# Fifteen small copies on GpSimd's queue are removed, and the hand-written order is replaced

## The chip, the cores and the metric

The kernel runs on one core of a Trainium2 chip. Such a core has a matrix engine (TensorE, PE in the profile; its weight loads are listed as PEld), three engines for elementwise work (VectorE = DVE, ScalarE = ACT, GpSimd = POOL), and SyncE (SP), which only issues transfers. Each engine takes its instructions strictly in order; engines and transfers meet only through semaphores. Transfers are issued by a queue (here POOL's, SP's and, at the very start and end, ACT's) and carried out by 16 DMA engines that all queues share. The metric is the device time of one execution in microseconds; lower is better.

## The reference

```python
B, H, S, D = 8, 12, 448, 64
scores = (q @ k.T) / sqrt(D)                  # per batch and head, 448 x 448
attn   = maximum(scores, 0) ** 2 / S          # no softmax
x      = (attn @ v) as [B*S, H*D]             # 3584 x 768
h      = x @ w_in                             # 768 -> 2048
g      = 0.5 * h * (1 + erf(h / sqrt(2)))     # exact gelu
out    = g @ w_out                            # 2048 -> 768, float32
```

All inputs are float32 in HBM; they are cast to bf16 on their way in by the transfers that POOL issues.

## The kernel before, in words

**Work.** Attention runs batch by batch (b = 0 to 7), each batch in three groups of four heads (g = 0, 1, 2), each group in seven steps of 64 keys (i = 0 to 6). One step is four matmuls `ps<-qT,kT` (L816), a relu `a_sq<-ps` (L828 on ACT or L830 on DVE) and a squaring `a_sq<-a_sq` (L838 on DVE). After the seven steps of a group come 28 matmuls `pav<-a_sq,v_sb` (L878) and two copies into `xT`. When all groups of a batch are done, the feed-forward part of that batch may start: `psh<-xT,win_sb` (L937) in 16 tiles of six matmuls for batches 0 to 3, a block form with fewer multiplications (`pb`, L1089) for batches 4 to 7, and `pso` (L1266) for the second layer of all. The feed-forward matmuls of earlier batches lie between the attention steps of later ones.

**How q and k arrive.** Scores need q and k transposed. For batches 0 and 1 TensorE does that (`tp`, L705 to L712). For batches 2 to 7 the path is: POOL issues a load of one group into `nq` (L511) or `nk` (L602); when it has landed SP issues a DMA transpose (L739) from `nq` into `qT`, or from `nk` into `kT`; for q the two halves of partitions are then also swapped into a second place, by DVE (two copies, L563) or by SP (two transfers, L760 and L761). `nq` and `nk` have four slots (NN = 4) and a batch takes three, so the load of a group overwrites a slot that a group of the batch before has used; `war` finds the transposes that must have read it.

**The gates.** `add_gate(b, g)` puts a copy of 128x16 values from `qT` to a tile `gate` that nobody reads on POOL (L784). It waits until the q transpose of group g of batch b has landed (for b = 2 until the swapped copy is made), and as POOL works in order, everything behind it in POOL's queue waits too. There are 15, for batches 2 to 6.

**What sets the order.** The string `ORDER` (L89) lists all work in one sequence: a letter for the engine (P = PE, A = ACT, D = DVE, G = POOL, S = SP) and the number of the operation in the order in which the program's text adds it; `Z1056` is a matmul of zeros, 1056 columns in all (L1601). `place` follows the list. So the list decides which engine does a relu, a copy or a swap where there is a choice, and in which order each engine's queue stands. The framework then adds the waits that the data need, and a wait of each POOL transfer for the eighth one ahead of it.

## Time and profile before

| | |
|---|---|
| median of 3 runs | 365.86 us (364.35 to 365.88) |
| the profiled execution | 366.48 us |
| its span, first to last instruction | 364.6 us |
| PE busy | 354.6 us (97%) |
| DVE busy | 297.8 us (82%) |
| ACT busy | 205.5 us (56%) |
| POOL busy | 67.0 us (18%) |
| granted TensorE clock | 1.00 |
| loads through POOL's queue | 22.47 MB, 42.8% of 16 DMA engines |
| SP's queue, transposes above all | 20.03 MB, 28.6% of 16 DMA engines |

The table is read from the first execution that the profiler recorded, which was 0.62 us longer than the median of the three runs. The share of an engine is a mean over stages that differ: until about 25 us TensorE waits for relus and copies, from there it is nearly always busy. The transfers of q, k and v go on until about 200 us; afterwards only outputs are stored.

### The profile page before, as it was taken

The page shows a single profiled execution, that of the slowest core. Times are in us where ns is not written, and L with a number is a line of the kernel's source. Part 1 is how long each engine was busy: PE and PEld are TensorE (multiplying, and loading weights), DVE is VectorE, ACT ScalarE, POOL GpSimd, SP SyncE. Part 2 cuts the span into 40 slices and gives each one's busy share as a digit, 9 for nine tenths or more (in the row PEclk, how much of TensorE's full clock was granted, in tenths as well). Part 3 has the DMA queues.
Part 4 walks back from the last instruction along what each step waited for, and adds up shares of the span by engine and source line. Part 5 has one row for each costly group of instructions (what it writes and reads, how often), then busy time and mean ns, then how long its engine had stood idle before and what let it go on. Part 6 is the DMA issues. An engine that isn't in the chain of part 4 may idle for free.

```text
span 364.6 us, 8274 instructions
## 1 busy us (share of the span) xinstructions
PE 354.6 (97%) x3439; PEld 222.0 (61%) x3439; DVE 297.8 (82%) x510; ACT 205.5 (56%) x333; POOL 67.0 (18%) x102
## 2 busy tenths in 40 slices
PE   8799999999999899999999999999999999999995
PEld 4464544555544455554455555899977887787663
DVE  3999878869999779999977999987866576767764
ACT  4999665546678585777966766425634025235000
POOL 8666173111723024052000000000000000000000
PEclk9999999999999999999999999999999999999999
DMA  9999999999899999999955301020101002402324
GB/s 175 201 200 200 184 172 178 191 197 207 134 173 177 144 232 166 196 173 224 192 132 72 91 2 45 2 62 27 42 6 43 2 8 80 131 0 61 99 58 131
DMA packets 72085, 43.87 MB, mean 120 GB/s; under 512 B 36336, under 2 KB 68720, under 8 KB 72048
## 3 DMA queue, kind: packets, MB, share of 16 engines
q0 software_dynamic: 32032, 22.47, 42.8%
q1 hardware_dynamic: 39120, 20.03, 28.6%
q10 hardware_dynamic: 896, 0.85, 0.7%
q8 instruction: 27, 0.44, 0.5%
q14 instruction: 10, 0.08, 0.1%
HBM read 45.61 MB, written 11.01 MB: 155 GB/s over the span
## 4 chain that ended last, share of the span: by engine, by line
PE 63%; DMA 21%; DVE 5%; ACT 4%; issue 3%; POOL 2%; SPq 0%; POOLq 0%; DVEq 0%
PE pso L1266 27%; PE pb L1089 18%; DMA nq<-in_q_dram 9%; PE psh L937 7%; DMA qT<-nq 7%; PE ps L816 5%; PE pav L878 4%; ACT a_sq L828 4%; DMA kT<-nk 4%; DVE a_sq L838 2%; DMA nk<-in_k_dram 2%; PE spin L1445 1%; DVE osb L1300 1%; DVE qT L563 1%; POOL wout_sb L532 1%
## 5 line engine op out<-in xcount | busy, mean ns | idle before, releaser
L828 ACT ACTIVATE a_sq<-ps 128x896 bf16<-128x896 f32 x126 | 110.5, 925 | 36.5 <-PE ps L816 36.2
L838 DVE TENSOR_TENSOR a_sq<-a_sq 128x896 bf16<-128x896 bf16 x169 | 96.4, 615 | 2.0 <-ACT a_sq L828 1.6
L937 PE MATMUL psh<-xT,win_sb 128*128 128x448 bf16 x384 | 76.9, 353 | 0.0
L830 DVE TENSOR_SCALAR a_sq<-ps 128x896 bf16<-128x896 f32 (+1 forms) x43 | 46.2, 1076 | 15.9 <-PE ps L816 15.6
L937 PEld LDWEIGHTS <-win_sb 128*128 128x128 bf16 x384 | 35.6, 98 | 38.2 <-issue 7.2
L1120 DVE TENSOR_TENSOR part<-pb,part 128x448 f32<-128x448 f32 x80 | 46.9, 619 | 12.9 <-PE pb L1089 11.1
L1266 PEld LDWEIGHTS <-s_sb 128*128 128x128 bf16 x424 | 40.4, 98 | 27.1 <-issue 3.3
L816 PE MATMUL ps<-qT,kT 64*64 64x448 bf16 (+1 forms) x700 | 47.8, 350 | 3.6 <-ACT a_sq L828 1.9
L947 ACT ACTIVATE h_sb<-psh 128x448 bf16<-128x448 f32 x64 | 34.5, 549 | 19.5 <-PE psh L937 19.5
L1266 PEld LDWEIGHTS <-h_sb 128*128 128x128 bf16 x312 | 29.9, 98 | 20.1 <-issue 2.3
L1089 PEld LDWEIGHTS <-win_sb 128*128 128x128 bf16 x384 | 36.9, 98 | 2.2
L1266 PE MATMUL pso<-t_sb,s_sb 128*128 128x384 bf16 x208 | 38.1, 326 | 0.0
L1266 PE MATMUL pso<-wout_sb,h_sb 128*128 128x384 bf16 x208 | 38.1, 326 | 0.0
L1266 PE MATMUL pso<-wout_sb,s_sb 128*128 128x384 bf16 (+1 forms) x208 | 37.7, 324 | 0.2 <-DVE osb L1300 0.2
L878 PE MATMUL pav<-a_sq,v_sb 64*64 64x448 bf16 (+1 forms) x700 | 36.1, 342 | 1.2 <-ACT a_sq L828 0.8
L1132 ACT ACTIVATE h_sb<-part 128x448 bf16<-128x448 f32 x48 | 25.2, 573 | 21.1 <-DVE part L1120 21.1
L816 PEld LDWEIGHTS <-kT 64*64 64x64 bf16 x700 | 18.3, 105 | 26.6 <-issue 18.1
L1300 DVE TENSOR_TENSOR osb<-pso,p_sb 128x384 f32<-128x384 f32 x39 | 21.5, 552 | 13.5 <-PE pso L1266 10.9
L878 PEld LDWEIGHTS <-v_sb 64*64 64x64 bf16 x700 | 20.9, 107 | 12.7 <-issue 2.2
L1089 PEld LDWEIGHTS <-ws 128*128 128x128 bf16 x288 | 27.7, 98 | 1.2
L1089 PE MATMUL pb<-xs,ws 128*128 128x224 bf16 x192 | 22.8, 259 | 0.0
L1089 PE MATMUL pb<-xs,win_sb 128*128 128x224 bf16 x192 | 22.5, 259 | 0.0
(70 smaller groups left out, 311.8 us busy)
## 6 DMA issues: line engine op xcount, KB each, us to landing
nk<-in_k_dram POOLq DMA_DIRECT2D x23, 224.0 KB, 8.1
nq<-in_q_dram POOLq DMA_DIRECT2D x23, 224.0 KB, 8.8
v_sb<-in_v_dram POOLq DMA_DIRECT2D x4, 672.0 KB, 8.9
out_dram<-osb SPq DMA_DIRECT2D x7, 336.0 KB, 3.8
v_sb<-in_v_dram POOLq DMA_DIRECT2D x10, 224.0 KB, 8.0
out_dram<-osb SPq DMA_DIRECT2D x7, 288.0 KB, 2.8
out_dram<-osb SPq DMA_DIRECT2D x8, 240.0 KB, 3.3
win_sb<-in_moe_w_in_dram POOLq DMA_DIRECT2D x8, 192.0 KB, 9.0
```

Of the source, the lines that this page charges most:

```text
L816: nc.tensor.matmul(ps[64 * j : 64 * j + 64, e, x * w : x * w + w], kT[r, g, i * 128 + 64 * j : i * 128 + 64 * j + 64], moving, start=True, ...
L828: A.activation(ar, ps, AF.Relu, scale=c_att)
L830: V.tensor_scalar(ar, ps, c_att, 0.0, op0=mybir.AluOpType.mult, op1=mybir.AluOpType.max,)
L838: V.tensor_mul(box["a2"][:, :, :used], ar, ar)
L878: nc.tensor.matmul(pav[0][o2 : o2 + 64, e, :w], get_v()[r, 2 * v_slot(b, g) + e, bass.ts(i, D)], box["a2"][r, y, o : o + w], start=(i == 0 ...
L937: nc.tensor.matmul(ph[:, x * n : x * n + n], win_sb[:, kd, bass.ts(m + x, 128)], xT[b][:, kd, c], start=(kd == 0), stop=(kd == KD - 1),)
L947: A.activation(h_ring()[:, m : m + nm, o + c.start : o + c.stop], box[0][:, :S].rearrange("p (x n) -> p x n", x=nm), AF.Gelu,)
L1089: nc.tensor.matmul(ps[name][:, z * HS : z * HS + HS], w[:, k, bass.ts(mm, 128)], right()[:, k], start=first and k == 0 and z == 0, stop=k ...
L1120: V.tensor_add(get(to), ps[name][:, :S], get(other))
L1132: A.activation(h_ring()[:, m : m + 2, o + half[c].start : o + half[c].stop], src().rearrange("p (x n) -> p x n", x=2), AF.Gelu,)
L1266: nc.tensor.matmul(box[bank][:, n0:n1], left()[:, kf], right()[:, kf, n0:n1], start=bool(need) and kf == 0, stop=kf == K2 - 1, skip_group_ ...
L1300: V.tensor_add(out()[:, n0:n1], box[bank][:, n0:n1], other()[:, n0:n1])
```

## The change

The function `add_gate`, its tile and its calls are removed, so POOL's queue holds loads alone (and the making of the identity matrix). A load still waits for the transposes that read the slot it overwrites. The numbers in `ORDER` shift by the 15 operations, and the list is also another one: on every engine much stands in another place, 33 relus go from ACT to DVE and 26 the other way, three swaps of q halves (batch 6 group 0, batch 7 groups 0 and 2) go from DVE to SP, two copies of transposed k of batch 0 go from DVE to ACT, and the matmul of zeros stands behind the first eight score operations instead of at PE's start.

```diff
 ORDER = """
-D13 G0 Z1056 A10 G1 G7 G4 A16 G108 G1461 P11 D12 P14 D15 P17 P29 P32 D18 P38 D39 P19 P21 A30 D20
...
+G0 A10 G1 G7 G108 A16 D13 G1446 P11 D12 P14 D15 P17 P29 A18 P32 A30 G3 P19 G4 A20 D33 P21 P35 P38
...
-    gate = const.tile([128, 16], BF16, tag="gate", name="gate")
-
-    def add_gate(b, g):
-
-
-        def fn(e):
-            nc.gpsimd.tensor_copy(gate, q_seg(b, 2 * g + (b == 2))[:, : SEG : SEG // 16])
-
-        deps = [Tq[b, g, 0][b == 2]]
-        pool_q.append(sch.add((("POOL", 0.2, 0.3),), fn, deps))
...
     add_T_dma(2, [[]] * 9)
-    add_gate(2, 0)
     add_wout(0)
     add_wout(1)
-    add_gate(2, 1)
     add_wout(2)
-    add_gate(2, 2)
...
                 for g in range(G):
-                    add_gate(b + 1, g)
                     add_load(b + 2, g, g + 1)
```

Three places show the new order. In the rows DMASW names the landing of a transfer that POOL issued, DMAHW of one that SP issued; DVE, PE, Activation and Pool are the engines' own counts.

**POOL, the loads of batch 4.** Before, from the gate for batch 3, group 2 to the k load of batch 4, group 1 (the last row); the big v load is that of batch 3:

```order
L784 COPY gate<-qT 128x16 [waits DMAHW4_49,Pool_49]
L620 DMA v_sb<-in_v_dram 128x6x448 [waits DMASW5_49,PE_49]
L602 DMA nk<-in_k_dram 128x2x448 [waits DMAHW0_49,DMASW6_49]
L784 COPY gate<-qT 128x16 [waits DMAHW3_49,Pool_49]
L511 DMA nq<-in_q_dram 112x4x256 [waits DMASW7_49,DMASW0_49]
L602 DMA nk<-in_k_dram 128x2x448 [waits DMAHW5_49]
L784 COPY gate<-qT 128x16 [waits DMAHW1_49,Pool_49]
L511 DMA nq<-in_q_dram 112x4x256 [waits DMASW1_49]
L784 COPY gate<-qT 128x16 [waits Pool_49]
L784 COPY gate<-qT 128x16 [waits DMAHW1_49,Pool_49]
L602 DMA nk<-in_k_dram 128x2x448 [waits DMAHW2_49,DMASW2_49]
```

The same stretch of the change, from the q load of batch 4, group 2 (which overwrites the slot of batch 3, group 1) to the v load of batch 4; the k load of batch 4, group 1 is the row before the last:

```order
L511 DMA nq<-in_q_dram 112x4x256 [waits DMAHW3_49,DMASW5_49,DMASW0_49]
L620 DMA v_sb<-in_v_dram 128x6x448 [waits DMASW6_49,PE_49]
L602 DMA nk<-in_k_dram 128x2x448 [waits DMAHW0_49,DMASW7_49]
L511 DMA nq<-in_q_dram 112x4x256 [waits DMAHW1_49]
L602 DMA nk<-in_k_dram 128x2x448 [waits DMAHW2_49,DMASW1_49]
L620 DMA v_sb<-in_v_dram 128x4x448 [waits DMASW2_49,PE_49]
```

The k load of batch 4, group 1 now stands behind loads alone; before, a gate for batch 4, group 0 stood right ahead of it.

**POOL, the first loads of batch 2.** Before, from a piece of `w_in` to the first gate; the first `nk` row is the k load of batch 2, group 0, the second that of group 1:

```order
L526 DMA win_sb<-in_moe_w_in_dram 128x3x512 [waits DMASW3_49]
L527 DMA win_sb<-in_moe_w_in_dram 64x3x512 [waits DMASW4_49]
L528 DMA win_sb<-in_moe_w_in_dram 64x3x512 [waits DMASW5_49]
L602 DMA nk<-in_k_dram 128x2x448 [waits DMASW6_49]
L602 DMA nk<-in_k_dram 128x2x448 [waits DMASW7_49,DVE_49,Activation_49]
L526 DMA win_sb<-in_moe_w_in_dram 128x3x512 [waits DMASW0_49]
L527 DMA win_sb<-in_moe_w_in_dram 64x3x512 [waits DMASW1_49]
L528 DMA win_sb<-in_moe_w_in_dram 64x3x512 [waits DMASW2_49]
L784 COPY gate<-qT 128x16 [waits DVE_49]
```

In the change the k load of batch 2, group 0 is the first row here, and the same piece of `w_in` comes behind it:

```order
L602 DMA nk<-in_k_dram 128x2x448 [waits DMASW5_49]
L620 DMA v_sb<-in_v_dram 128x2x448 [waits DMASW6_49]
L511 DMA nq<-in_q_dram 112x4x256 [waits DMASW7_49]
L526 DMA win_sb<-in_moe_w_in_dram 128x3x512 [waits DMASW0_49]
L527 DMA win_sb<-in_moe_w_in_dram 64x3x512 [waits DMASW1_49]
L528 DMA win_sb<-in_moe_w_in_dram 64x3x512 [waits DMASW2_49]
L602 DMA nk<-in_k_dram 128x2x448 [waits DVE_49,DMASW3_49,PE_49,Activation_49]
```

The k load of group 0 moves ahead of nine transfers: two pieces of `w_in` of three transfers each, two q loads and a v load. 30 transfers stood ahead of it in POOL's queue, now 21.

**ACT, the first relu of batch 2.** Its queue shows where PE's first score step of batch 2 stands, since each gelu `h_sb<-psh` follows one feed-forward tile on PE. Before, the relu of that step is the last row but one; thirteen gelus stand ahead of it in the whole queue:

```order
L947 ACTIVATE h_sb<-psh 128x448
L828 ACTIVATE a_sq<-ps 128x896
L947 ACTIVATE h_sb<-psh 128x448
L565 CAST xT<-pav 128x448 x2
L947 ACTIVATE h_sb<-psh 128x448 x6
L828 ACTIVATE a_sq<-ps 128x896 x2
L947 ACTIVATE h_sb<-psh 128x448
```

In the change the relu of the first step is DVE's, and that of the second step, which follows it directly on PE, is the `a_sq` row behind the two copies:

```order
L936 ACTIVATE h_sb<-psh 128x448
L817 ACTIVATE a_sq<-ps 128x896 x2
L936 ACTIVATE h_sb<-psh 128x448
L817 ACTIVATE a_sq<-ps 128x896
L565 CAST xT<-pav 128x448 x2
L817 ACTIVATE a_sq<-ps 128x896
L936 ACTIVATE h_sb<-psh 128x448
```

On PE ten feed-forward tiles stand ahead of the first score step of batch 2 instead of thirteen.

## The prediction

> **What bounds the kernel now.** I read the page first, then PE's waits, then the chain of waits, then the queues behind it. The page's first part, and the table of stretches:

> ```profile
> PE 354.6 (97%) x3439; PEld 222.0 (61%) x3439; DVE 297.8 (82%) x510; ACT 205.5 (56%) x333; POOL 67.0 (18%) x102
> ```
> ```profile
> 100.00:120.00 20.00, 20.00 (x197) 9.96 (x196) 19.58 (x34) 15.80 (x24) 5.94 (x9) 1.00 1.31 168
> 120.00:126.00 6.00, 4.70 (x52) 2.24 (x49) 4.72 (x8) 3.42 (x7) 0.00 (x0) 1.00 1.36 152
> 126.00:140.00 14.00, 13.99 (x134) 7.16 (x138) 10.61 (x18) 9.54 (x15) 5.43 (x9) 1.00 1.09 212
> 140.00:170.00 30.00, 29.55 (x318) 15.66 (x314) 28.86 (x51) 22.10 (x31) 7.88 (x15) 1.00 1.31 192
> 200.00:230.00 30.00, 29.84 (x309) 16.24 (x308) 29.79 (x56) 20.82 (x29) 0.00 (x0) 1.00 0.17 46
> ```

> After the stretch and its length the columns are PE, PEld, DVE, ACT and POOL busy, clock, DMA share. TensorE is the bound: 364.6 - 354.6 = 10.0 us idle in the whole span, at full clock. The change takes no matmul away, so it can gain only what PE idles or what PE spends thinly at the start. The one stretch with visible idle time in the middle is 120 to 126 us (1.30 us). DVE is the second bound: 1.14 us idle in 140 to 170, 0.21 us in 200 to 230. PE's waits:

> ```profile
> PE ps L816 <- ACT a_sq L828: 1.9, 5, 0.5
> PE ps L816 <- DMA kT<-nk: 1.3, 1, 1.3
> PE pav L878 <- ACT a_sq L828: 0.8, 2, 0.4
> PE pav L878 <- DVE a_sq L838: 0.4, 1, 0.4
> ```

> Columns: total us, times, longest. These are 4.4 of the 10.0 us; most of the rest lies ahead of the first matmul and behind the last, where only sums and stores are left. The chain of waits leads into the one DMA wait:

> ```profile
> 84.78 5.14 DMA qT<-nq
> ...
> 97.70 8.92 DMA qT<-nq
> ...
> 106.74 0.02 POOL gate L784
> 106.76 0.49 issue
> 107.25 5.71 DMA nk<-in_k_dram
> 112.97 0.02 issue
> 112.98 12.98 DMA kT<-nk
> ```

> Start, length. The gate for batch 4, group 0 waits for a transpose until 106.74; the k load of batch 4, group 1 stands behind it, lands at 112.96, its transpose at 125.97, and at 126.01 the first scores of that group start late.

> **The change part by part.** All terms are against the profiled execution's 366.48 us (span 364.6 us), 0.62 us above the median.

> *The gates themselves.* POOL's queue with two of them, before batch 4's loads:

> ```profile
> 90.04 3.42 POOL L784 COPY gate<-qT 128x16 bf16<-128x16 bf16 x1 [13.02 <-DMA qT<-nq]
> ...
> 106.74 0.24 POOL L784 COPY gate<-qT 128x16 bf16<-128x16 bf16 x1 [9.07 <-DMA qT<-nq]
> 107.25 0.70 POOL L602 DMA_DIRECT2D nk<-in_k_dram  x1 [0.27 <-issue]
> ```

> A copy of 0.2 us on an engine that is 18% busy costs PE nothing; what counts is the idle time in brackets, in which POOL issued no load.

> *The wait at 126 us.* In the new queue the k load of batch 4, group 1 stands behind loads that wait for transposes of batch 3, the last of which lands near 90 us (84.78 + 5.14 = 89.92). With four more loads ahead at about 0.7 us of issue each it goes out near 94 instead of 107.25. Its transpose then lands 13 us earlier, near 113 at the same lengths. PE wants it at 124.7 (126.01 - 1.30) or some 2 us sooner, since the new list puts three fewer tiles ahead of it. Ten us of cover: the wait goes. Gain 1.3 us, between 0 (if what follows waits instead) and 1.74, the wait of the weight load of the same step:

> ```profile
> 126.01 0.14 PEld L816 LDWEIGHTS <-kT 64*64 64x64 bf16 x8 [1.74 <-DMA kT<-nk]
> ```

> *What is late next.* Time gained at 126 has to be kept up by DVE. It has 3.39 us to spare in 126 to 140, then almost none to 170. The new list gives DVE seven relus more on balance and takes three swaps (two copies each), two copies of kT and six copies to xT from it:

> ```profile
> L830 DVE TENSOR_SCALAR a_sq<-ps 128x896 bf16<-128x896 f32 x42 | 45.5, 1086 | 15.5 <-PE ps L816 15.2
> L563 DVE COPY qT<-qT 64x896 bf16<-64x896 bf16 x28 | 12.1, 434 | 2.3 <-DMA qT<-nq 1.6
> L563 DVE CAST xT<-pav 128x448 bf16<-128x448 f32 x8 | 4.8, 616 | 0.3 <-ACT xT L565 0.3
> L563 DVE COPY kT<-tp 128x896 bf16<-128x896 bf16 x5 | 3.1, 616 | 0.0
> ```

> 7 x 1.09 = 7.6 against 6 x 0.43 + 2 x 0.6 + 6 x 0.62 = 7.5 us: an even exchange over the run, but the copies of kT leave the first 10 us, so about 1.2 us more come later. Where DVE has no idle time that lands on PE. Of the 1.3 us I take 0.5 back; bounds 0 and 1.2 + 1.1 = 2.3 (the later work, and DVE's idle time of 140 to 170 if it has to fall somewhere).

> *The swaps on SP.* Three more swaps are two transfers each on SP (0.5 to 0.6 us of issue) and make SP wait for the transpose ahead of them:

> ```profile
> 179.43 0.55 SPq L760 DMA_DIRECT2D qT<-qT  x1
> 180.03 0.59 SPq L761 DMA_DIRECT2D qT<-qT  x1
> ...
> 186.18 175.41 SPq L1220 DMA_DIRECT2D out_dram<-osb x44
> ```

> Behind them stand later transposes of batches 6 and 7. Before, SP is through with all transposes at 186.1, when PE is still in batch 6 (by its place in the list, the step at 197.70 in the rows of the chain below is the first of batch 7). Three swaps at 1.1 us plus a landing of about 5 us (the 5.14 above) push them by 8 at most: cost nothing, cover 10 us.

> *The start of batch 2.* This is the tightest place, because the new list wants it sooner. Rows of SP, PE and the weight loads:

> ```profile
> 32.52 1.32 SPq L739 DMA_TRANSPOSE qT<-nq  x1
> 40.59 3.14 SPq L739 DMA_TRANSPOSE kT<-nk  x2
> ```
> ```profile
> 32.52 10.79 DMA qT<-nq
> ```
> ```profile
> 49.00 0.33 PEld L816 LDWEIGHTS <-kT 64*64 64x64 bf16 x12 [0.37 <-DMA kT<-nk]
> ```
> ```profile
> 126.58 1.24 PE psh L937 x6
> ...
> 172.33 3.52 PE psh L937 x18
> ...
> 197.70 0.69 PE ps L816 x12
> ```

> Now the scores of batch 2 start at 49.00, just as the transpose of k lands (0.37 us wait). A feed-forward tile is 3.52 / 3 = 1.17 us; with three fewer ahead, and small moves besides, PE comes there near 45.1. The k load moves up by nine transfers, so its transpose no longer waits for the load until 40.59; it follows that of q, at 33.8. If both take the 10.8 us that the q transpose took among loads, k lands at 44.6: no wait. If the second adds a further 2 us to the first, 46.6: 1.5 us wait. I take 0.6 us; bounds 0 and 3.9 (k lands at 49 as now). [...]

> *The first microseconds.*

> ```profile
> 4.70 0.62 ACT L565 CAST nq<-q 112x512 bf16<-112x512 f32 x1 [1.44 <-DMA q<-in_q_dram]
> ...
> 7.32 1.73 ACT L828 ACTIVATE a_sq<-ps 128x896 bf16<-128x896 f32 x2 [1.59 <-PE ps L816]
> ```
> ```profile
> 5.13 0.64 PE L1601 MATMUL fill<-zero 64*64 64x512 bf16 x3
> 5.69 0.37 PE L705 MATMUL tp<-ident,nq 112*128 112x112 bf16 x4
> ```

> Without the zeros at the start the first transposes begin when the cast ends, 5.32 instead of 5.69: 0.37 us. ACT then works without a break, as in 15 to 20 us:

> ```profile
> 15.00:20.00 5.00, 3.91 (x79) 2.39 (x82) 4.80 (x10) 5.00 (x10) 3.52 (x5) 1.00 1.39 196
> ```

> It gets two copies of kT (about 0.4 and 0.8 us); the first fits into its 1.59 us of waiting, the second does not, but one half copy to xT (about 0.4 us) leaves. Sum -0.37 + 0.8 - 0.4: 0. I take -0.2 for one more score step done by then (0.19 us); bounds -0.6 and +0.8.

> *Changes between attention and feed-forward on PE.* A tile by itself takes 1.24 us and one of a row of three 1.17 (both in the rows of the chain above), so three single tiles take 0.2 us more than a row of three, which has two pairs of changes fewer: about 0.1 us a pair. The list has 89 changes instead of 87, one pair more: +0.1.

> *Sum.* -1.3 + 0.5 + 0 + 0.6 - 0.2 + 0.1 = -0.3 us on 366.48, so 366.2; less 0.62, about **365.6 us** as a median. I call anything within 0.5% (1.8 us) no change, about what a measurement of this kernel can tell.

> **The rivals.**
> *Faster: the new list also fits better.* Without gates the loads have more room, and a list made for that may close the other small waits too. For it: the ten us of cover at 126. Against it: the two long rows of PE's waits are for ACT and DVE, which loads don't touch. The price: the 1.3 us kept in full and half of the 1.9 + 0.8 + 0.4 us: 1.3 + 1.6 = 2.9, so 363.0.
> *Slower: loads stretch the transposes.* The gates kept loads off while transposes ran (5.14 us); beside loads they take 8.92 to 12.98. At batch 2 there is no slack at all: if k's transpose lands no sooner than now, PE waits 3.9 us instead of the 0.6 in my sum, 365.6 + 3.3 = 368.9. It decides from a landing later than about 47.5. Against it: the k load is moved up by about 9 us. [...]
> *Slower: DVE takes over.* If the 2.3 us of its upper bound land on PE: 365.6 + 1.8 = 367.4, and with an uneven exchange between 140 and 230 us more, about 368.
> *No effect: a load takes the gate's place.* POOL is in order, and the new queue has early loads that wait for transposes too: the k load of batch 3, group 1 waits for that of batch 2, group 0, where the first gate stood. Then the loads start again when they did; 365.9, inside my forecast.

> **How the numbers follow.** No change (mine and the last rival) 0.37; faster 0.31; slower by the transposes 0.20; slower by DVE 0.12. The likeliest, 365.6, is the prediction. Its own range is 364.1 to 367.6. For 8 in 10 it reaches to the faster rival, 362.7, and to the slower one, 368.9.

> **What would show it.** Right: no PE wait for kT near 124 us, the k load of batch 4, group 1 out before 100 us, DVE above 95% from 126 to 170, first scores of batch 2 between 45 and 47 us with a wait under 1.5 us, the last transpose before 195 us. Wrong: PE waits of several us for kT or qT of batch 2 or 6, waits for DVE of more than 2 us in sum, or a first feed-forward tile (27.2 us now) that moves by more than 1 us.

## The result and the profile after

| | before | after |
|---|---|---|
| median of the runs, us | 365.03 (22 runs) | 366.60 (22 runs) |
| lowest and highest, us | 364.24, 365.88 | 365.14, 371.94 |
| profiled execution, us (its span) | 366.48 (364.6) | 368.19 (366.4) |

The ratio after to before is 1.0047, with a 95% interval from 1.0027 to 1.0068: slower by half a per cent, where 0.2% faster (365.6 us) was forecast. The time lies inside the range of 362.7 to 368.9. This ratio leaves out the runs more than 1.5% above the fastest of their kernel, five here, though these turn out below to be the kernel's own doing. The spread is the first thing to see: the kernel before stays within 1.7 us, the changed one takes 365.1 to 366.7 us in 13 runs and 368.2 to 371.9 in the other 9.

The first part of the page after, the stretches that the prediction showed (the same columns: stretch, length, PE, PEld, DVE, ACT and POOL busy, clock, DMA share, GB/s) with one more, 45 to 50 us:

```profile
PE 355.9 (97%) x3439; PEld 221.1 (60%) x3439; DVE 298.6 (82%) x504; ACT 204.2 (56%) x333; POOL 59.8 (16%) x87
```
```profile
45.00:50.00 5.00, 4.17 (x60) 1.80 (x62) 4.27 (x9) 3.88 (x7) 1.90 (x3) 1.00 1.24 153
100.00:120.00 20.00, 20.00 (x199) 10.00 (x196) 18.85 (x32) 13.99 (x23) 4.07 (x6) 1.00 1.44 142
120.00:126.00 6.00, 5.90 (x60) 2.71 (x54) 5.56 (x10) 3.91 (x7) 1.64 (x3) 1.00 1.42 134
126.00:140.00 14.00, 13.20 (x116) 6.48 (x116) 12.28 (x20) 10.44 (x17) 1.35 (x2) 1.00 1.32 219
140.00:170.00 30.00, 29.38 (x312) 15.47 (x316) 27.62 (x47) 19.83 (x27) 9.01 (x13) 1.00 1.23 200
200.00:230.00 30.00, 30.00 (x314) 15.92 (x307) 28.59 (x52) 22.32 (x32) 0.84 (x1) 1.00 0.36 77
```

TensorE now idles visibly at 45 to 50 us (0.83) and about 126 to 141 us; DVE has more room than before in 140 to 170 and 200 to 230 us. TensorE's waits (total us, times, longest) say for what:

```profile
PE ps L805 <- DMA kT<-nk: 2.3, 3, 1.1
PE ps L805 <- ACT a_sq L817: 1.2, 3, 0.4
PE ps L805 <- DVE qT L563: 1.1, 2, 0.8
PE pav L867 <- ACT a_sq L817: 0.4, 1, 0.4
```

The waits for ScalarE have shrunk (1.9 to 1.2, and 0.8 to 0.4). In their place stand three waits for a transpose of k instead of one, and two waits of 1.1 us in all for DVE's copies of q; these two lie at 9.4 and 15.3 us, in the new early list, and the kernel before has neither. The rows of the three waits on TensorE (start, length, the wait in brackets) are the first scores of batch 2, of batch 4, group 1, and of batch 5:

```profile
47.62 0.57 PE L805 MATMUL ps<-qT,kT 64*64 64x448 bf16 x8 [0.83 <-DMA kT<-nk]
...
126.29 0.57 PE L805 MATMUL ps<-qT,kT 64*64 64x448 bf16 x8 [0.30 <-DMA kT<-nk]
...
140.62 0.57 PE L805 MATMUL ps<-qT,kT 64*64 64x448 bf16 x8 [1.14 <-DMA kT<-nk]
```

The chain of waits now runs through DMA from 33.7 us on. First piece: the transpose of k of batch 2, group 0, and POOL let go by it. Second piece: loads and transposes of batch 4.

```profile
33.72 13.85 DMA kT<-nk
47.57 0.02 issue
47.59 0.02 POOLq L602
47.61 0.49 issue
48.10 0.73 POOL nk L602
48.83 6.35 DMA nq<-in_q_dram
```
```profile
93.14 12.62 DMA nk<-in_k_dram
105.76 0.02 issue
105.78 1.22 SPq L739
...
113.88 12.37 DMA kT<-nk
126.24 0.04 issue
126.29 0.60 PE ps L805 x8
```

POOL's queue shows what took the gates' place (start, length, idle time ahead; first the gate for batch 2, group 0 before, then the rows after):

```profile
44.20 0.65 POOL L784 COPY gate<-qT 128x16 bf16<-128x16 bf16 x1 [8.53 <-DVE qT L563]
```
```profile
48.10 0.73 POOL L602 DMA_DIRECT2D nk<-in_k_dram  x1 [8.98 <-DMA kT<-nk]
...
91.60 0.73 POOL L511 DMA_DIRECT2D nq<-in_q_dram  x1 [14.37 <-DMA qT<-nq]
...
94.57 0.73 POOL L602 DMA_DIRECT2D nk<-in_k_dram  x1
...
107.65 0.71 POOL L511 DMA_DIRECT2D nq<-in_q_dram  x1 [11.58 <-DMA qT<-nq]
```

POOL issues in order, so a load that overwrites a buffer holds everything behind it until the transpose that reads the buffer has landed: 8.98, 14.37 and 11.58 us, where the gates held 8.53, 13.02 and 9.07. The first hold ends at 48.1 instead of 44.2 us, and the loads behind it land two to three us later than those behind the gate did. The k load of batch 4, group 1 goes out at 94.57, as forecast, but lands only at 110.18, with five other loads and three transposes beside it; its own transpose takes 12.37 us beside the loads of batch 5 and lands at 126.24, where it landed at 125.97 before.

### The profile page after: what moved, and what is told of

The parts are those of the page before. It is cut to its first block, busy times and chain, and to the rows that moved or that the text cites. A ratio compares the mean times of both kernels' runs of the same rounds, so it can differ in the third digit from the quotient of the medians.

```text
span 366.4 us, 8257 instructions
## 1 busy us (share of the span) xinstructions
PE 355.9 (97%) x3439; PEld 221.1 (60%) x3439; DVE 298.6 (82%) x504; ACT 204.2 (56%) x333; POOL 59.8 (16%) x87
## 4 chain that ended last, share of the span: by engine, by line
PE 65%; DMA 22%; ACT 5%; SPq 4%; issue 2%; DVE 1%; POOL 1%; POOLq 0%
PE pso L1255 29%; PE pb L1078 18%; DMA nq<-in_q_dram 9%; DMA kT<-nk 8%; PE psh L926 6%; PE ps L805 5%; PE pav L867 4%; ACT a_sq L817 4%; DMA nk<-in_k_dram 3%; SPq L739 3%; DMA qT<-nq 2%; PE spin L1434 1%; SPq L1209 1%; DVE a_sq L827 1%; POOL wout_sb L532 1%
## 5 line engine op out<-in xcount | busy, mean ns | idle before, releaser
L817 ACT ACTIVATE a_sq<-ps 128x896 bf16<-128x896 f32 (+1 forms) x119 | 105.0, 928 | 28.5 <-PE ps L805 28.1
L819 DVE TENSOR_SCALAR a_sq<-ps 128x896 bf16<-128x896 f32 (+1 forms) x50 | 53.8, 1078 | 16.7 <-PE ps L805 16.3
L1109 DVE TENSOR_TENSOR part<-pb,part 128x448 f32<-128x448 f32 x80 | 46.9, 618 | 17.2 <-PE pb L1078 17.0
L1255 PEld LDWEIGHTS <-s_sb 128*128 128x128 bf16 x424 | 40.3, 98 | 27.2 <-issue 3.0
L805 PE MATMUL ps<-qT,kT 64*64 64x448 bf16 (+1 forms) x700 | 48.1, 350 | 5.0 <-DMA kT<-nk 2.3
L1078 PEld LDWEIGHTS <-ws 128*128 128x128 bf16 x288 | 27.7, 98 | 1.2
L511 POOL DMA_DIRECT2D nq<-in_q_dram x24 | 17.7, 739 | 54.0 <-DMA qT<-nq 40.6
L602 POOL DMA_DIRECT2D nk<-in_k_dram x23 | 16.6, 725 | 36.7 <-issue 17.8
```

What stands on the lines that cost most here:

```text
L805: nc.tensor.matmul(ps[64 * j : 64 * j + 64, e, x * w : x * w + w], kT[r, g, i * 128 + 64 * j : i * 128 + 64 * j + 64], moving, start=True, ...
L817: A.activation(ar, ps, AF.Relu, scale=c_att)
L819: V.tensor_scalar(ar, ps, c_att, 0.0, op0=mybir.AluOpType.mult, op1=mybir.AluOpType.max,)
L1078: nc.tensor.matmul(ps[name][:, z * HS : z * HS + HS], w[:, k, bass.ts(mm, 128)], right()[:, k], start=first and k == 0 and z == 0, stop=k ...
L1109: V.tensor_add(get(to), ps[name][:, :S], get(other))
L1255: nc.tensor.matmul(box[bank][:, n0:n1], left()[:, kf], right()[:, kf, n0:n1], start=bool(need) and kf == 0, stop=kf == K2 - 1, skip_group_ ...
```

## The experiments

Theory after the two traces: the loss is made ahead of 50 us, at the first scores of batch 2, which the new list sets where the transpose of k lands, with loads beside it. Rival: it is made at batches 4 and 5, where the same happens with smaller waits. In the diffs a line is an entry of one engine's queue in words.

### The old order without gates

```diff
 POOL's queue of the kernel before, all else the same
-gate batch 2, group 0        (and the 14 other gates)
 load v of batch 1, group 2
```

> The order before, word for word, with its 15 gates taken out and nothing else moved. Only four of the gates held POOL before (8.53, 13.02, 9.07 and 15.50 us). Theory (a gate kept loads off the transposes): the loads behind the first gate go out near 36 us instead of 44.8, run beside the transposes of batch 2, the transpose of its first k lands 1 to 4 us after 48.8, and TensorE waits there; the wait at 126 us goes or shrinks by at most 1.3. Time 365.0 + 2 - 1 = 366, between 365.5 and 368. Rival (the gates cost something and protected nothing): the wait at 126 us goes, nothing else changes, 363.7.

Measured: 371.6 us (5 runs, 369.6 to 372.2), ratio 1.0168 (1.0143 to 1.0193). TensorE's rows:

```profile
51.27 0.76 PE L804 MATMUL ps<-qT,kT 64*64 64x448 bf16 x12 [1.53 <-DMA kT<-nk]
...
61.05 0.94 PE L804 MATMUL ps<-qT,kT 64*64 64x448 bf16 x8 [2.06 <-DVE qT L562]
62.55 0.38 PE L804 MATMUL ps<-qT,kT 64*64 64x448 bf16 x4 [0.56 <-DVE a_sq L818]
```

The transpose of k of batch 2, group 0 lands at 51.2 instead of 48.8 us, that of q of group 1 at 60.5 instead of 52.3 (the swap of its halves on DVE follows, and TensorE waits 2.06 us for it). The theory has the direction and the place right, but not the size: the time lies above its range of 365.5 to 368, a loss of 6.8 us where about 1 was expected. The three waits shown are 4.2 us of it in an execution of 369.8 us at a mean granted clock of 0.999; the other four executions had 0.995. Near 126 us TensorE waits no more. The rival is out: at least one gate protected something.

### One gate left

```diff
 POOL's queue of the kernel before
 gate batch 2, group 0
-the 14 other gates
```

> The order before with one gate left of the 15, that of batch 2, group 0. Without any gate this order took 6 us more, and its trace shows them at 51 to 63 us (first scores of batch 2), while the wait at 126 us was gone and TensorE lost 1.9 us less than before between 65 and 220 us. Theory (only the first gate protects anything; the others cost): 365.0 - 1.5 = 363.5, between 363.0 and 364.5, faster than before. Rival (the later gates are worth as much as they cost): 365.0, between 364.5 and 366.

Measured: 365.68 us (12 runs), ratio 1.0022 (0.9994 to 1.005). The theory is out and the rival's range holds: the first gate is worth the whole 6 us of this order. Taking the other fourteen out wins nothing, although TensorE has no wait for a transpose at 126 us in this profile. Whether they save a little is open: the median is 0.8 us above that of the kernel before beside it (364.92), but the interval includes no change.

### The kernel before once more

> The kernel before a second time, for a second profile of it: the prediction's largest term rests on one wait at 126 us in one execution. Theory: the wait belongs to the kernel and is there again, 1 to 2 us at the first scores of batch 4, group 1; time 365. Rival: it differs from one execution to the next, and is under 0.5 us here.

Measured: 365.51 us, span 363.7. The same stretch and the same steps (first the stretch, then TensorE's rows):

```profile
120.00:126.00 6.00, 6.00 (x64) 3.10 (x63) 5.42 (x10) 3.52 (x7) 0.00 (x0) 1.00 1.26 178
```
```profile
123.88 1.50 PE L882 MATMUL pav<-a_sq,v_sb 64*64 64x448 bf16 x28
125.21 0.72 PE L820 MATMUL ps<-qT,kT 64*64 64x448 bf16 x8
125.86 1.31 PE L941 MATMUL psh<-xT,win_sb 128*128 128x448 bf16 x6
```

The rival holds: there is no wait at all. The transpose landed at 124.3 instead of 125.97, ahead of the scores' turn at 125.21. The wait of 1.3 us, on which the largest term of the prediction rests, was in one of the two profiled executions of this kernel and not in the other.

### Half of one order, half of the other

```diff
 all five queues, cut at the first scores of batch 3 (about 85 us)
-old order with its gates throughout
+first run:  old order with its gates, then the new order without
+second run: the new order without gates, then the old order with its later gates
```

> The order before with its gates up to the first scores of batch 3, the new order without gates from there. Theory (the loss is made ahead of 50 us: first feed-forward tile at 28.26 instead of 27.23, and 1.2 us more wait at the first scores of batch 2; later on the two orders come out even, 0.25 us in favour of the new one): 364.6, between 364.0 and 365.3. Rival (the loss is the loads beside the transposes of batches 4 and 5): 366 or more.

> The other half: the new order without gates up to the first scores of batch 3, the order before from there, with the gates that stand behind that point. Theory (loss ahead of 50 us): 366.8, between 366.2 and 367.5. Rival (loss at batches 4 and 5): 365.2.

Measured: old then new 365.96 us, ratio 1.0037 (1.0023 to 1.0051); new then old 368.33 us (6 runs, 367.3 to 372.4), ratio 1.0122 (1.0083 to 1.0162). Both times are above the theory's, the first one at the rival's edge, but most of the loss goes with the new early half. In the first run there is no wait for a transpose at all, so the new late half does without gates when the early half comes on time; its one wait of a us is at the seam, for ScalarE at 102.83 us (1.02 us). What the seam of the second run costs was not separated. The second run was profiled in an execution of 372.38 us, and the place of the loss stands in it open to see:

```profile
50.68 0.96 PE L820 MATMUL ps<-qT,kT 64*64 64x448 bf16 x8 [4.19 <-DMA kT<-nk]
51.57 2.42 PE L941 MATMUL psh<-xT,win_sb 128*128 128x448 bf16 x6
```

TensorE waits 4.19 us for the same transpose, which lands at 50.63 here and not at 47.57; behind that wait a feed-forward tile takes 2.42 us instead of 1.31.

A later cut was tried for a version that might beat both kernels.

> The order before with its gates up to the first scores of batch 4, group 1 (about 124 us), the new order without gates from there. In the profiles so far TensorE loses 2.1 us (before, second profile) behind 105 us in the old order and 1.4 us in the new one, where the loads came on time. Theory (the late half of the new order is a little better, since DVE is waited for less; only its first 105 us are worse): 365.0 - 0.7 = 364.3, between 363.7 and 364.9. Rival (the two halves don't fit at the seam, as in the other run that was cut, where ScalarE was waited for 1.2 us at 103 us): 365.5 or more.

Measured: 366.65 us, ratio 1.0061 (1.0046 to 1.0077). The rival holds: at the seam, 130 to 134 us, TensorE waits for ScalarE and DVE (0.83 and 0.64 us in its rows). Two lists that were each balanced as a whole don't fit in the middle.

### The new order with three gates

```diff
 POOL's queue of the changed kernel
+gate batch 2, group 0
 load v of batch 1, group 2
 load w_in, last quarter
 ...
+gate batch 3, group 2
 load v of batch 3
 ...
+gate batch 4, group 0
 load k of batch 4, group 1
```

> The new order with three of the four gates that held POOL put back, each ahead of the load that it stood ahead of (batch 2 group 0, batch 3 group 2, batch 4 group 0; in the new order the fourth, of batch 5 group 2, has no such place, since its transpose stands behind the k load that the gate would hold). Theory: the first gate lets the transposes of batch 2 land sooner (45 to 46 instead of 47.57), which takes about 1 us off the wait there, but the v load and the last quarter of w_in behind it come at 51 to 54 us, about when PE wants them; the gate of batch 4 sends the k load of group 1 out at 107 instead of 94.57, so PE's wait near 126 grows by 0 to 2. Sum about 0: 366.6, between 365.6 and 368. Rival (the lost gates are the whole loss): 365.0 or less.

Measured: 370.43 us, ratio 1.0166 (1.0141 to 1.0192), above the theory's range; the rival is out. About 1.1 us of it is probably not the gates': the first feed-forward tile comes at 29.4 us instead of 28.3, before any gate holds a load (the expectation of the second run on the first scores of batch 2, below, says why). The transpose of k lands at 44.21, and nothing waits for it. But the gate waits for the swap on DVE until 46.5, and what stands behind it is late:

```profile
51.92 1.52 PE L881 MATMUL pav<-a_sq,v_sb 64*64 64x448 bf16 x28 [1.77 <-DMA v_sb<-in_v_dram]
...
56.64 3.57 PE L940 MATMUL psh<-xT,win_sb 128*128 128x448 bf16 x18 [1.39 <-DMA win_sb<-in_moe_w_in_dram]
```

So loads held back do bring the transpose 3.4 to 6.4 us forward, and the new list has no room for the loads that are held. Both waits stand behind the first gate; the new order with that gate alone was not run.

### First scores of batch 2 later

```diff
 TensorE's queue of the changed kernel
 product with v of batch 1, group 1
+feed-forward tile 10 of batch 0
+feed-forward tile 9 of batch 0
 scores of batch 2, group 0: steps 0 and 2
-feed-forward tile 10 of batch 0
```

> The changed kernel with the first scores of batch 2 put back by two feed-forward tiles (2.3 us; tiles 10 and 9 of batch 0 go ahead of them, the product with v of batch 1, group 2 two steps further up, tile 13 one step up; their gelus move along on ScalarE). Nothing else moves; no load, no transpose. Theory (the place has no slack: the transpose of k lands at 47.6 in one profile and about 50.6 in another, and a wait there also halves TensorE's clock for some us): the wait of 1.0 to 4.4 us shrinks by 2.3, no run at a low clock is left or few, median 365.6, between 365.0 and 366.2. Rival (the relus come 2.3 us later and TensorE waits for them instead): 366.6 as before the edit, or more.

Measured: 368.36 us (4 runs), but with the first feed-forward tile at 29.2 us: the buffers that TensorE writes to (PSUM) had been dealt out in another order, and the run says little. The same two tiles moved without that, with the product and tile 13 left where they were:

> The run on the first scores of batch 2 again. In that run (and in the one with gates in the new order) the buffers of PSUM were dealt out in another order, and the first feed-forward tile came at 29.2 to 29.4 us instead of 28.0 to 28.6, which has nothing to do with the edit; here they are dealt out as in the changed kernel. Tiles 10 and 9 of batch 0 go ahead of the first scores of batch 2 on TensorE, and their gelus with that of tile 2 ahead of the relu on ScalarE; nothing else. Theory (no slack at this place): the wait of 1.0 to 4.4 us shrinks by 2.3, hardly a run at a low clock, median 365.6, between 365.0 and 366.2. Rival (relus 2.3 us later are missed later): 366.6 or more.

Measured: 367.3 us (9 runs, 366.1 to 371.2), ratio 1.0082 (1.0051 to 1.0113). In the profiled execution of 366.61 us there is no wait for a transpose left anywhere, but a wait for DVE of 0.82 us at 51.01; and three of the nine runs still take 369 us and more. Neither theory nor rival is right alone: the wait for the transpose goes, and the relus that come later are missed. In this profile k landed at 47.26; that two tiles are not enough where it lands near 50 is likely for the long runs, two of which had a clock of 0.993 and 0.994, but none of them was profiled.

### A load moved, no gate

```diff
 POOL's queue of the changed kernel
 load v of batch 1, group 2
+load k of batch 3, group 1     (waits for the transpose of k of batch 2, group 0)
 load w_in, last quarter
-load k of batch 3, group 1
```

> The changed kernel with the load that holds POOL (k of batch 3, group 1, which waits for the transpose of k of batch 2, group 0) moved ahead of the last quarter of w_in, so that this quarter no longer runs beside that transpose; the three feed-forward tiles that need the quarter (13 and 12 of batch 0, 13 of batch 1) go behind five others, with one half copy to xT a step earlier. No gate. Theory (the loads beside the transposes of batch 2 make the loss, and the later waits at batches 4 and 5 follow from POOL being let go late): the transpose of k lands at 44 to 46 us instead of 47.6 to 50.6, POOL goes on 2 to 5 us sooner, the wait at 47 us is gone, no run at a low clock; median 365.2, between 364.5 and 366.0. Rival (the waits at batches 4 and 5 are independent and take what is gained at batch 2): 366.6, between 366.1 and 367.

Measured: 368.52 us (6 runs, 367.0 to 370.5), ratio 1.0087 (1.0057 to 1.0118). The transpose lands at 45.49 (first row, from the chain: start and length) and the wait at 47 us is gone, as the theory says; but the time lies above even the rival's 366.1 to 367. All six runs had a clock of 1.00, so their spread of 3.5 us is not the clock's. The loads behind the quarter of w_in land later, and TensorE waits at two other places:

```profile
33.73 11.76 DMA kT<-nk
```
```profile
73.21 0.57 PE L819 MATMUL ps<-qT,kT 64*64 64x448 bf16 x8 [1.74 <-DMA kT<-nk]
...
141.19 0.57 PE L819 MATMUL ps<-qT,kT 64*64 64x448 bf16 x8 [1.27 <-DMA kT<-nk]
```

What was taken from one transpose came back at two others, as far as the one profile (369.06 us) shows.

### Zeros ahead of batch 2

```diff
 TensorE's queue of the changed kernel
 product with v of batch 1, group 1
+4800 columns of zeros (2 us)
 scores of batch 2, group 0: step 0
```

> The changed kernel with 2 us of multiplications by zeros (4800 columns) on TensorE right ahead of the first scores of batch 2; they do no needed work, they only fill the wait. Theory (a long wait there lets TensorE's clock fall to half, and that makes the runs of 368 to 372 us): filled, no run falls to a low clock; runs that waited 1 us lose about 1 us, runs that waited long gain some; all between 366 and 369, median 367.3, clock 0.998 or more. Rival (the clock falls for another reason, or the long runs have another cause): a third or more of the runs stay above 369, at clock 0.995 or less, and the median goes up by the full 2 us to 368.6.

Measured: 366.7 to 371.8 us in 6 runs, median 368.24. By the times this is not decided: three runs are still over 369, one of them at a low clock (0.995). The profiled execution says more:

```profile
50.42 0.57 PE L819 MATMUL ps<-qT,kT 64*64 64x448 bf16 x8 [1.30 <-DMA kT<-nk]
50.92 1.31 PE L940 MATMUL psh<-xT,win_sb 128*128 128x448 bf16 x6
```

The transpose lands as late as in the long executions (50.38), but TensorE was idle for 1.30 us only, and the tile behind it takes its usual 1.31 us. So the slow tile goes with the wait and not with the late transpose. The execution is long all the same (369.07 us): the zeros and the wait together take 3.3 us there, as long as the long waits.

### The changed kernel three times more

> The changed kernel a second time, for a second profile. Theory: the transpose of k of batch 2, group 0 lands between 47.5 and 50.7 us; if below 48.5, TensorE waits about 1 us there, waits again at batches 4 and 5, and the time is near 366; if above 50, it waits over 3 us, its matmuls take twice as long for some us behind that wait, the later waits are gone, and the time is 368 to 372. Rival (the long runs have no tie to this transpose): a time over 368 with a landing below 48.5, or one under 367 with a landing above 50.

> The changed kernel unedited, for a third profile. Theory: in an execution of about 366 us the transpose of k of batch 2, group 0 lands near 47.5, TensorE waits about 1 us for it, and the waits at batches 4 and 5 (0.95 and 1.3 us in the first profile) are mostly absent; TensorE loses 3 to 3.7 us in all behind the first feed-forward tile, against 2.8 before. Rival: the waits at batches 4 and 5 are there and the one at batch 2 is not.

> The same once more, since which kind an execution is of can't be chosen. Theory: time over 368 goes with a landing over 49.5 us or with both waits at batches 4 and 5; time near 366 with a landing near 47.5 and without them. Rival: no such tie.

Measured: five runs of 366.2 to 370.3 us (ratio 1.0073, 1.0039 to 1.0107), profiled at 370.33; then 367.74 and 370.01. The first scores of batch 2 and the tile behind them, in the third profile (367.74 us), the fourth (370.01) and the second (370.33):

```profile
49.16 0.57 PE L805 MATMUL ps<-qT,kT 64*64 64x448 bf16 x8 [2.30 <-DMA kT<-nk]
49.66 1.31 PE L926 MATMUL psh<-xT,win_sb 128*128 128x448 bf16 x6
```
```profile
49.82 0.60 PE L805 MATMUL ps<-qT,kT 64*64 64x448 bf16 x8 [3.21 <-DMA kT<-nk]
50.35 2.42 PE L926 MATMUL psh<-xT,win_sb 128*128 128x448 bf16 x6
```
```profile
50.12 0.57 PE L805 MATMUL ps<-qT,kT 64*64 64x448 bf16 x8 [3.26 <-DMA kT<-nk]
50.62 2.01 PE L926 MATMUL psh<-xT,win_sb 128*128 128x448 bf16 x6
```

| execution | k of batch 2 lands | wait | tile behind it | waits at 126 and 141 us | us |
|---|---|---|---|---|---|
| first profile | 47.57 | 0.83 | 1.31 | 0.30, 1.14 | 368.19 |
| third | 49.11 | 2.30 | 1.31 | none | 367.74 |
| fourth | 49.77 | 3.21 | 2.42 | none | 370.01 |
| second | 50.08 | 3.26 | 2.01 | none | 370.33 |
| new order, then old | 50.63 | 4.19 | 2.42 | none (old late list) | 372.38 |

The tie holds with one exception that its expectation counted for the rival: 368.19 us with a landing at 47.57, the execution in which the two later waits exist. In the other three profiles of the changed kernel the transpose for 126 us lands at 119.6 to 120.7 instead of 126.24: the k load goes out and lands nearly as before (108.6 to 109.9 instead of 110.18), but its transpose takes 5.9 to 7.9 us instead of 12.37. The next loads in POOL's queue go out at 111.6 to 113.3 us there and at 107.65 in the first profile, so fewer run beside it; that this is the cause is not shown by an edit. Nor is it shown why the transpose of batch 2 lands at 47.6 in one execution and at 50 in the next. An execution of 366.0 us was never caught with a profile; from this table the transpose should land at 47.5 or sooner there and the later waits be missing too, but that is not shown. So the about 1 us that the short runs lose has no profile of its own.

None of these versions beats the kernel before.

## Why the prediction was wrong, step by step

*The wait at 126 us (-1.3): the step that failed.* The prediction took 1.3 us off for a wait that only one of the two profiles of the kernel before has. The mechanism came in part: the k load went out at 94.57, near the forecast 94. But "at the same lengths" was wrong: the load took 15.61 us instead of 5.71, and its transpose landed at 126.24 in the first profile, 119.6 in the second. And as a rule the gain was not there to be had: the second profile (365.51 us) has no wait at this place. The profiled execution of 366.48 us was 0.62 us above the median of the three runs shown, above all three, and is 1.45 above the median of the 22 (365.03). This excess was taken off at the end as if both kernels had it, while the wait that was to be gained is of the same size as the excess (1.3 and 1.45). From 365.03 and without this term the sum gives 366.0, where 366.60 was measured; the rest is in the next step.

*The start of batch 2 (+0.6; bounds 0 and 3.9): the mechanism was right, the size was off.* TensorE came to the first scores at 46.5 to 46.9 us (47.62 - 0.83 and so on) and waited 0.83, 2.30, 3.21, 3.26 and 4.19 us; the forecast had it there at 45.1 with a wait of 0.6. The estimate gave the second transpose the 10.8 us of the first, or 2 more. It took 13.85 to 16.52, though the first one took only 9.3 in the first profile. SP issued the second 1.4 us behind the first there (33.72 and 32.30), and each was priced as if it were alone; measured are 15 to 18 us for the pair. All five landings, 47.57 to 50.63, lie past the 47.5 from which the slower rival decides, and none of the five executions shows the wait of 0.6: the shortest is 0.83. The upper bound was too low as well: behind the waits of over 3 us TensorE ran at half its clock for some us (0.50 in the execution of 372.38 us, see the last section). From the first scores of batch 2 to the third feed-forward stretch behind them it takes 3.95 us in the first and third profile, and 5.53, 5.58 and 6.27 us behind the three long waits: 1.6 to 2.3 us more.

*What is late next (+0.5): wrong in sign.* From 145 to 330 us TensorE idles for 0.61 and 0.34 us in the two profiles of the kernel before and for 0.00 in all four of the changed kernel. Its waits for ScalarE in the whole run fall from 2.7 or 2.8 us to 1.5 or 1.6, and behind 16 us none for DVE is left. DVE was busy for 91% of 126 to 170 us in the first profile, where above 95% was the sign. So a few tenths were gained where a loss was put down.

*The swaps on SP (0): right.* The last transposes of batch 7 land at 196 to 199 us in the four profiles, a little behind the mark of 195, and no score of batches 6 and 7 waits.

*The first microseconds (-0.2): nothing.* With the new early list the first feed-forward tile comes at 28.0 to 28.6 us in eight profiles, with the old one at 27.2 to 28.3 in six, with two score steps less (0.38 us) ahead of it. On the means (28.3 and 27.7) that leaves about +0.15 us, inside what one execution differs from the next. (The first profiles alone, 28.26 against 27.23, would have met the sign of being wrong.)

*Changes on PE (+0.1).* No run isolates this term.

*The gates themselves (0).* As an instruction a gate costs nothing: right. What a gate protects was not priced. Eleven of the fifteen hardly held POOL (0.31 us at most), taking fourteen out wins nothing, and the first is worth 6 us in the old order.

*The rivals.* "Loads stretch the transposes" came true at its own place and its own point, a landing later than about 47.5 us; 368.9 lies among the long executions, and the short ones lose about 1 us. "A load takes the gate's place" came true as well: the k load of batch 3, group 1 held POOL for 8.98 us. It was put down as harmless, but it holds POOL behind the last quarter of w_in, not ahead of it, so the transposes had loads beside them and POOL was let go 4 us later. The chance of 0.20 on the first was too small: at the tightest place of the list all hung on a transpose, and the trace showed lengths from 3 to 15 us. "DVE takes over" did not come, nor did "faster", though the smaller waits it spoke of did shrink. The range's lower end, 362.7, does not follow from that rival's own price, which gives 363.0.

## What to carry to other kernels

A wait that is seen in one profiled execution is worth its size only if it is there in the next one: where a prediction rests on one wait of a us, look first at how far the profiled execution stands above the median. Another order on an in-order queue moved the hold here and did not remove it; ask which loads go out ahead of the hold and run beside the transfer that someone waits for. Price two transfers that follow each other in one queue as a pair: here the pair took 15 to 18 us, and its second half was the one that was waited for.

## What the runs showed of the hardware

```profile
46.00:48.00 2.00, 0.48 (x12) 0.05 (x4) 1.39 (x3) 1.39 (x3) 0.00 (x0) 1.00 1.82 183
48.00:50.00 2.00, 0.00 (x0) 0.00 (x0) 0.00 (x0) 0.00 (x0) 0.00 (x0) 0.70 1.02 64
50.00:51.00 1.00, 0.32 (x4) 0.19 (x8) 0.00 (x0) 0.00 (x0) 0.00 (x0) 0.50 2.89 113
...
55.00:56.00 1.00, 1.00 (x20) 0.57 (x16) 1.00 (x1) 0.48 (x1) 1.00 (x2) 0.68 1.37 183
```

The clock is at half from 48.8 to 55.6 us there, worked out from the 0.70 and the 0.68 of that column. Over 45 to 57 us its mean is 0.72 in this execution and 0.86 in those of 370.33 and 370.01 us, which at half clock makes stretches of about 6.7, 3.4 and 3.4 us (an estimate); in the first and third profile, with waits of 0.83 and 2.30 us, it is 1.00 over the same time. The clock did not fall at a fixed time into a wait: in the execution of 372.38 us it fell 2.3 us into it (46.5 to 48.8), while in that of 370.33 us the first scores behind a wait of 3.26 us still took 0.57 us, as in the first profile, and only the tile behind them was slow (2.01 instead of 1.31). What sets the moment of the fall and the length of the stretch is not shown.

That made a late transfer dearer here than its delay, and it goes with two groups of times. Of the changed kernel's 22 runs the 13 short ones had a mean clock of 0.998 or more, seven of the nine long ones 0.991 to 0.995; the other two (368.19, the first profile, and 369.05) are long at 0.998 and 0.999, so the clock is not all of it. Of some 80 runs of the kernel before, where TensorE's rows show no wait there in either profile, one was above 366.7 us.

TensorE's pace changes at the start too: the eleven multiplications by zeros take 4.21 us in one execution of the kernel before and 4.88 in the next. In the first the spacing of these matmuls falls from 0.427 to 0.218 us at 4.4 us; in the second they take as long as in the first profile of the changed kernel (4.88 us), where the spacing stays at 0.427 up to the last of them:

```profile
0.99 4.21 PE L1445 MATMUL spin<-zero 128*128 128x512 bf16 x11 [0.99 <-DVE zero L1428]
```
```profile
0.99 4.88 PE L1449 MATMUL spin<-zero 128*128 128x512 bf16 x11 [0.99 <-DVE zero L1432]
```

Half a us at the start of this kernel is therefore chance: TensorE's first transposes begin at 5.69 us in the first and at 6.37 in the second.
